# The order in which a weight's norm products take its converted blocks

## The chip, the cores and the metric

The kernel runs on one core of a Trainium2 chip. The metric is the device time of one execution in microseconds, lower is better. Engines are named as in the profile: PE (TensorE, with PEld for its weight loads), DVE (VectorE), ACT (ScalarE), POOL (GpSimd) and SP (SyncE, which issues the DMAs). Each engine works through its own queue of instructions in order.

## The reference

Three stages follow one another. The first is attention that keeps, for each query, the 32 highest scores; the second and the third are two feed-forward layers on its output. The inputs are: q, k, v of 4 batches x 8 heads x 576 tokens x 64; w_gate and w_val 512 x 1536, w_out 1536 x 512, w_in 512 x 2048, w_out2 2048 x 512.

```
scores = q @ k^T / 8;  kept where >= the 32nd largest of the row, else -1e9
attn   = softmax(scores) @ v          -> x, 2304 tokens x 512
x      = (sigmoid(x @ w_gate) * (x @ w_val)) @ w_out
out    = (max(x @ w_in, 0) ** 2) @ w_out2
```

## The kernel before

**Tiling.** The 2304 tokens are 18 tiles of 128 rows, in eleven chunks: four of one tile and seven of two. Attention goes by chunk, by pair of heads, by head and by tile. For each such block PE makes the scores (L281), ACT copies them out of PSUM (L284), DVE finds the 32 largest in four rounds of a maximum and a replacement (L294, L300), POOL and ACT make the masked exponential (L304 to L308), and PE transposes it (L338 or L340) and multiplies it with the values (L373).

**The weights.** They arrive as float64. A weight is cut into blocks of 128 x 512, and two blocks make a pair (6 pairs each for w_gate, w_val and w_out, 8 each for w_in and w_out2; 34 pairs, 68 blocks). `conv` turns a pair into float32: ACT L447 and L466, DVE L461 and L462, POOL L467. When a weight's pairs are there, `scale` looks for a power of two by which the weight can be scaled. It multiplies every 128 columns, cut to bfloat16, with themselves and adds all of that up in one PSUM tile (L484, eight products for each pair, called "the products" below; the trace names the PSUM tile wg_n, wv_n, wo_n, wi_n and, for w_out2, w_n). Then DVE takes the diagonal (L490), PE spreads its sum over the partitions (L492), DVE takes the maximum (L493), and four small DVE steps turn it into the scale. The PSUM tile is one of the two buffers named "wk", which the feed-forward layers' products use too. `split` (L502 to L508) uses the scale to cut the float32 pair into two float16 parts.

**Who needs the result.** Chunk 0 goes through the two layers in plain float32 (`moe32`, L745 to L833) and needs no scale. The other chunks need the split parts (`moe`, L593, L633, L696, L717).

**What sets the order.** The program is written with a priority for each piece of work: attention comes first, then the plain chunk, then the weights' conversions. When the program is built, a planner lays out the instruction order of every engine from these priorities, the dependencies and its own estimated times. On the chip that order is fixed, and each instruction waits on semaphores for what it needs. For w_gate, w_val and w_out `scale` is called right behind the last `conv` of the weight; for w_in and w_out2 it is called between steps of the plain chunk.

Of the kernel before, what the change touches and what calls it, by code (L numbers as in the profile page):

```python
# [19 lines left out]
DRAM = bass.MemoryType.DRAM  # L20

P = 128
# [40 lines left out]
LOA = 0  # L63
# Operands of the split products are scaled by powers of two so that their
# column norms lie below 2**TB; the scales are undone exactly afterwards.
TB = 15
# [3 lines left out]
def tile_topk_attention__then__two_moe_layers(  # L70
# [11 lines left out]
    chunks=None,  # L82
# [7 lines left out]
    KM = DM // P  # L90
# [27 lines left out]

# [1 line left out]
    def pow2_scale(norm, name, pool=mpool, tag=None, bufs=None, squared=True):  # L120
# [13 lines left out]

# [1 line left out]
    kscr = {}  # L136
    kloc = {}

    def prep_keys(b, hp, keep=False):
        """Of two heads: k^T in two parts, each part's rows the heads' one after the other."""  # L140
        src = k[b, 2 * hp : 2 * hp + 2]
        kn = apool.tile([P, S], F32, tag="kn", bufs=1, name=f"kn_{b}_{hp}")
        kv = kn[:, 0 : CB * P].rearrange("p (c h d) -> p c h d", c=CB, h=2)
        for j in range(2):
            nc.sync.dma_start(kv[:, :, j], src[j, 0:SM].rearrange("(p c) d -> p c d", c=CB))
        ke = apool.tile([ST, 2, D], F32, tag="qn", bufs=2, name=f"ke_{b}_{hp}")
        nc.sync.dma_start(ke, src[:, SM:S].rearrange("h p d -> p h d"))
        kh = apool.tile([P, S], F32R, tag="kst", bufs=KST, name=f"kp_{b}_{hp}")
        kl = kn.bitcast(F32R)
        if keep:  # L150
            kl = mpool.tile([P, S], F32R, tag="m4", bufs=M4, name=f"kl_{b}_{hp}")
            kloc[(b, hp)] = (kh, kl)
        for lo, hi in ((0, CB), (CB, NB)):
            pt = ps_t.tile([P, 512], F32, tag="tr", name=f"kpt_{b}_{hp}_{lo}")
            w = 0
            for c in range(lo, hi):
                kp = P if c < CB else ST
                nc.tensor.transpose(
                    pt[:, w : w + kp],
                    (kv[:, c] if c < CB else ke).rearrange("p h d -> p (h d)"),  # L160
                    ident[0:kp, 0:kp],
                )
                w += kp
            c0 = lo * P
            nc.scalar.copy(kh[:, c0 : c0 + w], pt[:, 0:w])
            nc.vector.tensor_tensor(
                kl[:, c0 : c0 + w], pt[:, 0:w], kh[:, c0 : c0 + w], op=ALU.subtract
            )
        d = dpool.tile([2, 2, D, S], F32R, name=f"ks_{b}_{hp}", tag=f"ks_{b}_{hp}")
        for a, t in enumerate((kh.bitcast(F32), kl.bitcast(F32))):  # L170
            for j in range(2):
                nc.sync.dma_start(d.bitcast(F32)[j, a], t[j * D : (j + 1) * D])
        for j in range(2):
            kscr[(b, 2 * hp + j)] = d[j].rearrange("a d s -> (a d) s")

# [1 line left out]
    def pieces(tt):  # L177
# [21 lines left out]
    class Pair:  # L199
        """Two heads of one chunk of tokens."""  # L200

# [37 lines left out]
        def queries(self, tts):  # L239
            for tt in tts:  # L240
# [8 lines left out]
                for b, _, o, n in ps:  # L249
                    # tokens of another batch are zero here  # L250
                    qt = apool.tile([P, 2, 2, P], F32R, tag="qt", bufs=3, name=f"qt_{tt}_{self.hp}_{b}")
                    for p_b, _, o_, n_ in ps:
                        if p_b != b:
                            nc.gpsimd.memset(qt.bitcast(F32)[:, :, :, o_ : o_ + n_], 0.0)
                    sl = slice(o, o + n)
                    nc.scalar.copy(qt[:, 0, :, sl], p3[:, :, sl])
                    nc.vector.tensor_tensor(
                        qt[:, 1, :, sl], p3[:, :, sl], qt[:, 0, :, sl], op=ALU.subtract
                    )
                    self.qt[(tt, b)] = qt  # L260

        def scores(self, j, i):
# [5 lines left out]
            for e in range(2):  # L268
                half = slice(e * HALF, (e + 1) * HALF)
                ops = []  # L270
                for b, _, _, _ in ps:
                    for a in range(2):
                        if self.ci == 0:
                            # both parts still on chip, each head's on its own partitions
                            rows = slice(j * D, (j + 1) * D)
# [11 lines left out]
        def softmax(self, j, i, ss):  # L287
# [26 lines left out]
            if self.ci < DIAG:  # L314
                dg = apool.tile([P, P], F32, tag="we", bufs=3, name=f"dg_{tt}_{h}")
                nc.gpsimd.tensor_scalar(dg, ident, rz, 1.0, op0=ALU.mult, op1=ALU.mult)
                return wk, dg
            # the last keys of both heads lie side by side, to be transposed at once
            if j == 0:
# [5 lines left out]
        def transpose(self, j, i, wk, dg):  # L325
# [8 lines left out]
            for c in range(CB):  # L334
                o, x = tp[:, c * P : (c + 1) * P], wk[:, c * P : (c + 1) * P]
                if self.ci < DIAG:
                    # normalized on the way
                    nc.tensor.matmul(o, x, dg, start=(c == 0), stop=(c == CB - 1), skip_group_check=True)  # L338
                else:
                    nc.tensor.transpose(o, x, ident)  # L340
# [41 lines left out]

# [1 line left out]
    # A float64 weight arrives as its two 32-bit words. The high word, read as a float32,  # L384
    # has the float64's exponent divided by 8 as its own and the rest of it in its mantissa:
    # times 2**-112 it has float32's exponent (what is too small for it becomes zero or next
    # to it), only 3 bits too low. Shifted up, and with its sign and the 3 highest bits of
    # the low word put in, it is the float32.
    REBIAS = float(2.0**-112)
# [10 lines left out]
    nblk = [0]  # L400
    flat = {}  # (name, kt, fb): float32 tile of two blocks, index
    sums = {}
    parts = {}  # (name, kt, fb): tile, index
    scales = {}
# [21 lines left out]
    def conv(name, pi):  # L426
        """Two blocks to float32, and the norms' share of them."""
        pr = pairs_of[name][pi]
# [19 lines left out]
        if wide:  # L448
            for e, r in enumerate(rs):
                hi = r[:, :, 1]  # L450
                if SGN and nblk[0] % SGN == 0:
                    # a zero of the same sign
                    nc.gpsimd.tensor_scalar(
# [20 lines left out]
    def scale(name):  # L474
        """Of a whole weight, from the Gram matrices of its columns, cut to bfloat16, 128 columns
        at a time, all added up: no column's squared norm is above the diagonal's largest entry."""
        gram = ps_w.tile([P, 512], F32, tag="wk", name=f"{name}_n")[:, 0:P]
        n = 0
        for pr in pairs_of[name]:
            c = flat[(name, *pr[0])][0]  # L480
# [56 lines left out]
    def split_act(src, name, xs, N):  # L537
        # src: [P, KM, N]; columns' largest squared norm gives the scale
        sq = xs[:, 1].bitcast(BF16)
# [19 lines left out]

# [1 line left out]
    class Moe:  # L561
# [4 lines left out]
    def start(ci):  # L566
        """The gate and value products of a chunk's first features, ahead of their turn."""
        m = ahead[ci]
# [45 lines left out]
    def moe(ci, nxt=None):  # L614
        """nxt: called before and after the turn from the first layer to the second."""
        m = ahead.pop(ci)
# [3 lines left out]
        def l1_acc(fp, gh):  # L620
            if not accs:
                accs.append(ps_a.tile([P, 2, 512], F32, tag="acc", name=f"acc1_{ci}"))
            acc = accs[0]
            # the last ones bank by bank
            last = fp == NF1 // 2 - 1
# [53 lines left out]
        usc, i2 = layer2_scales()  # L679
        # out = acc2 * (1/(scale of r))**2 / (scale of w_out2)  # L680
        us = mpool.tile([P, 2], F32, tag="us", bufs=2, name=f"us_{ci}")
# [7 lines left out]
        def l2_pair(fp):  # L689
            ph = ps_w.tile([P, 512], F32, tag="wk", name=f"ph_{ci}_{fp}")  # L690
            for e in range(2):
                f0 = (2 * fp + e) * P
                # the low parts of x2 last
                terms = [(c, a, 0) for c in range(KM) for a in range(2)] + [(c, 0, 1) for c in range(KM)]
# [43 lines left out]

# [1 line left out]
    def moe32(ci, xt):  # L740
# [47 lines left out]
        l1_acc(*prev)  # L788
        x2 = xt  # no longer needed
        nc.scalar.copy(x2.rearrange("p d n -> p (d n)"), accs[0][:, 0, 0 : KM * N])  # L790
# [44 lines left out]

# [1 line left out]
    def batches(ci):  # L837
# [9 lines left out]
    up = [0]  # L847

    def attention():
        """Yields once for each block of 128 rows of one head."""  # L850
        units = []
# [44 lines left out]
        def tail(n):  # L896
            pr, pi, j, i = units[n]
            if pr.hp == 0 and pr.ci not in xts:
# [6 lines left out]
                else:  # L905
                    # of a small chunk, its split parts lie in the same tile
                    small = pr.ci in SM2
# [28 lines left out]
    def layer2_scales():  # L936
        if not usc:
            # 1/(scales of w_val, w_out, w_in) and the fixed powers of two between them
            u = const.tile([P, 1], F32, name="usc")
# [25 lines left out]

    # the parts each weight is split into once the plain chunks are done with it
    todo = []  # (least number of steps of the last plain chunk, weight, pair)
    n1 = NF1 // 2
# [109 lines left out]
```

## Time and profile before

| | us |
|---|---|
| median of 3 runs | 1314.05 |
| lowest and highest run | 1313.09, 1314.7 |
| span of the profiled execution, first to last instruction | 1312.3 |
| PE busy in it | 1214.3 (93%) |
| DVE busy | 1018.8 (78%) |
| POOL busy | 838.6 (64%) |
| ACT busy | 758.5 (58%) |
| mean granted TensorE clock | 0.969 of full speed |

The span is that of one profiled execution; the median is 1.75 us above it, and this is taken as what lies around the span. A share of the whole span mixes two stages with different limits, so the stretches are to be read one by one.

### The profile page before, as it was taken

The page shows a single profiled execution, that of the slowest core. Times are in us where ns is not written, and L with a number is a line of the kernel's source. Part 1 is how long each engine was busy: PE and PEld are TensorE (multiplying, and loading weights), DVE is VectorE, ACT ScalarE, POOL GpSimd, SP SyncE. Part 2 cuts the span into 40 slices and gives each one's busy share as a digit, 9 for nine tenths or more (in the row PEclk, how much of TensorE's full clock was granted, in tenths as well). Part 3 has the DMA queues.
Part 4 walks back from the last instruction along what each step waited for, and adds up shares of the span by engine and source line. Part 5 has one row for each costly group of instructions (what it writes and reads, how often), then busy time and mean ns, then how long its engine had stood idle before and what let it go on. Part 6 is the DMA issues. An engine that isn't in the chain of part 4 may idle for free.

```text
span 1312.3 us, 28283 instructions
## 1 busy us (share of the span) xinstructions
PE 1214.3 (93%) x10613; PEld 971.6 (74%) x10613; DVE 1018.8 (78%) x2192; ACT 758.5 (58%) x1500; POOL 838.6 (64%) x1124
## 2 busy tenths in 40 slices
PE   6746798989999899999999999999999999999998
PEld 4535686777978778777888678777876887787775
DVE  6999999999999999989899888985998698210010
ACT  4876767677666665666566655664566566323122
POOL 1988878888676675586567746674576557324223
PEclk9766899999999999999999999999999999999999
DMA  6967861221323221524211233321111110000000
GB/s 187 350 246 252 276 206 56 62 64 54 94 67 103 61 62 28 132 70 137 82 53 36 73 101 96 95 67 53 42 48 42 46 37 10 17 2 1 17 1 16
DMA packets 116328, 113.00 MB, mean 86 GB/s; under 512 B 73440, under 2 KB 87776, under 8 KB 116192
## 3 DMA queue, kind: packets, MB, share of 16 engines
q1 hardware_dynamic: 116192, 111.19, 28.3%
q8 instruction: 84, 1.38, 0.4%
q14 instruction: 52, 0.43, 0.1%
HBM read 96.99 MB, written 14.16 MB: 85 GB/s over the span
## 4 chain that ended last, share of the span: by engine, by line
PE 70%; DVE 14%; POOL 6%; ACT 3%; DMA 3%; issue 3%; SPq 1%; ACTq 0%; POOLq 0%; DVEq 0%
PE acc L717 13%; PE ph L696 12%; PE pg L593 9%; PE pv L593 9%; PE acc L633 9%; PE xp L373 6%; PE sp L281 6%; PE tp L340 4%; DVE mx L294 3%; DVE W L300 3%; POOL W L307 1%; PE qpt L244 1%; DMA wv_r<-in_moe_w_val_dram 1%; DVE wv_c L462 1%; POOL W L322 1%
## 5 line engine op out<-in xcount | busy, mean ns | idle before, releaser
L294 DVE MAX8 mx<-W 128x8 f32<-128x576 f32 x432 | 327.4, 758 | 7.7
L307 POOL TENSOR_TENSOR W<-S,W 128x576 f32<-128x576 f32 x144 | 208.1, 1445 | 32.6 <-ACT W L306 32.1
L696 PE MATMUL ph<-x,wi_w 128*128 128x256 f16 (+1 forms) x1920 | 209.2, 260 | 8.0 <-ACT x L672 7.4
L300 DVE MATCH_REPLACE8 W<-mx,W 128x576 f32<-128x576 f32 x288 | 213.7, 742 | 0.0
L717 PE MATMUL acc<-w_w,rh 128*128 128x512 f16 x816 | 195.8, 379 | 1.5 <-POOL rh L709 1.5
L696 PEld LDWEIGHTS <-wi_w 128*128 128x128 f16 x1920 | 167.2, 99 | 39.7 <-issue 10.4
L306 ACT ACTIVATE W<-S,bs 128x576 f32<-128x576 f32 x144 | 112.0, 778 | 108.2 <-POOL bs L304 107.9
L593 PE MATMUL pg<-xs,wg_w 128*128 128x256 f16 (+1 forms) x1440 | 156.0, 257 | 3.1 <-ACT xs L547 1.6
L308 ACT ACTIVATE W<-W,bs 128x576 f32<-128x576 f32 x144 | 112.0, 778 | 71.8 <-POOL W L307 71.3
L593 PE MATMUL pv<-xs,wv_w 128*128 128x256 f16 (+1 forms) x1440 | 152.7, 257 | 0.2 <-DVE x2cm L668 0.2
L281 PE MATMUL sp<-kst,qt 128*128 128x288 f32 x608 | 130.6, 327 | 9.0 <-ACT S L284 5.0
L593 PEld LDWEIGHTS <-wg_w 128*128 128x128 f16 x1440 | 122.4, 98 | 18.3 <-issue 2.7
L633 PEld LDWEIGHTS <-wo_w 128*128 128x128 f16 x1440 | 123.1, 98 | 16.6 <-issue 3.7
L593 PEld LDWEIGHTS <-wv_w 128*128 128x128 f16 x1440 | 122.7, 98 | 16.4 <-issue 3.3
L717 PEld LDWEIGHTS <-rh 128*128 128x128 f16 x816 | 77.7, 98 | 76.4 <-POOL rh L709 2.0
L605 DVE TENSOR_TENSOR th<-pv,th 128x512 f32<-128x512 f32 (+1 forms) x60 | 36.2, 603 | 119.1 <-PE pv L593 117.9
L633 PE MATMUL acc<-gh,wo_w 128*128 128x256 f16 (+1 forms) x1200 | 124.8, 254 | 2.4 <-POOL gh L609 2.4
L294 DVE MAX8 mx<-S 128x8 f32<-128x576 f32 x144 | 107.4, 746 | 15.7 <-ACT S L284 15.4
L708 POOL TENSOR_TENSOR r<-r 128x512 f32<-128x512 f32 (+1 forms) x80 | 74.7, 936 | 59.8 <-ACT rh L707 58.8
L341 ACT COPY PT<-tp 128x512 f32<-128x512 f32 x144 | 83.7, 581 | 47.6 <-PE tp L340 39.3
L322 POOL TENSOR_SCALAR we<-W,rz 128x64 f32<-128x64 f32 x128 | 41.5, 324 | 108.0 <-DVE rz L313 72.7
L300 DVE MATCH_REPLACE8 W<-mx,S 128x576 f32<-128x576 f32 x144 | 106.8, 742 | 0.3 <-issue 0.3
(297 smaller groups left out, 2224.8 us busy)
## 6 DMA issues: line engine op xcount, KB each, us to landing
kst<-ks SPq DMA_DIRECT2D x104, 288.0 KB, 2.9
v<-in_v_dram SPq DMA_DIRECT2D x112, 128.0 KB, 2.2
qn<-in_q_dram SPq DMA_DIRECT2D x128, 64.0 KB, 2.2
wi_r<-in_moe_w_in_dram SPq DMA_DIRECT2D x16, 512.0 KB, 6.8
w_r<-in_moe_w_out_dram SPq DMA_DIRECT2D x16, 512.0 KB, 4.7
wg_r<-in_moe_w_gate_dram SPq DMA_DIRECT2D x12, 512.0 KB, 8.0
wv_r<-in_moe_w_val_dram SPq DMA_DIRECT2D x12, 512.0 KB, 7.2
wo_r<-in_moe_w_out_dram SPq DMA_DIRECT2D x12, 512.0 KB, 7.0
```

What stands on the lines that cost most here:

```text
L281: nc.tensor.matmul(sp[:, e, 0:HALF], l, r, start=(x == 0), stop=(x == len(ops) - 1))
L294: m8 = nc.vector.max(mx[:, r], cur)
L300: nc.vector.match_replace(wk, mx[:, r], cur, NEG)
L306: nc.scalar.activation(wk, ss, AF.Relu, bias=bs[:, 0:1], scale=-BIG)
L307: nc.gpsimd.tensor_tensor(wk, ss, wk, op=ALU.subtract)
L308: nc.scalar.activation(wk, wk, AF.Exp, bias=bs[:, 1:2], scale=SCALE, accum_out=bs[:, 2:3])
L341: nc.scalar.copy(ptr[:, :, i * P : (i + 1) * P], tp.rearrange("p (c t) -> p c t", c=CB))
L373: nc.tensor.matmul(xp[j * D : (j + 1) * D, o : o + n], vj, pj, start=(si == 0 and c == 0), stop=(c == NB - 1), skip_group_check=True,)
L593: nc.tensor.matmul(pp[:, e * N : (e + 1) * N], wblk(wd, a, c, f0, P), xs[:, b_, c, :], start=(e == 0 and n == 0), stop=(n == 3 * KM - 1), ...
L633: nc.tensor.matmul(acc[:, d // 2, (d % 2) * N : (d % 2 + 1) * N], wblk("wo", a, f, d * P, P), gh[:, b_, e * N : (e + 1) * N], start=(f == ...
L696: nc.tensor.matmul(ph[:, e * N : (e + 1) * N], wblk("wi", a, c, f0, P), x2[:, b_, c, :], start=(e == 0 and n == 0), stop=(n == 3 * KM - 1) ...
L717: nc.tensor.matmul(acc2[:, i, 0:DM], gh[:, b_, e * N + i * P : e * N + (i + 1) * P], wblk("w2", a, f, 0, DM), start=(f == 0 and x == 0), s ...
```

## The change

`scale` walks the pairs of a weight from the last to the first. The products, their number, their operands and their sum's place are the same; the first of a weight's products now reads the pair that is converted last. All other lines of the diff remove comments.

```
     def scale(name):
         gram = ps_w.tile([P, 512], F32, tag="wk", name=f"{name}_n")[:, 0:P]
         n = 0
-        for pr in pairs_of[name]:
+
+        for pr in reversed(pairs_of[name]):
             c = flat[(name, *pr[0])][0]
             m = c.bitcast(BF16).rearrange("p e (f t) -> p (e f) t", t=2)[:, :, 1]
             for f in range(1024 // P):
                 mf = m[:, f * P : (f + 1) * P]
                 nc.tensor.matmul(
                     gram, mf, mf, start=(n == 0), stop=(n == len(pairs_of[name]) * (1024 // P) - 1)
                 )
                 n += 1
```

## Rows read from the trace of the kernel before

**Rows 1.** Stretches: length, busy time (instructions) of each engine, granted clock, DMA.

```profile
core 0: us, PE busy (x) PEld busy (x) DVE busy (x) ACT busy (x) POOL busy (x), PEclk, DMA share, GB/s
27.00:250.00 223.00, 163.55 (x1195) 132.82 (x1195) 216.16 (x375) 158.67 (x300) 188.11 (x159) 0.84 0.64 217
66.00:100.00 34.00, 15.77 (x102) 11.77 (x103) 34.00 (x56) 24.82 (x48) 30.46 (x23) 0.60 0.67 244
...
300.00:1312.00 1012.00, 989.43 (x8765) 786.01 (x8763) 737.52 (x1684) 553.63 (x1114) 606.70 (x902) 1.00 0.20 57
```

**Rows 2.** What PE waited for from 27 to 150 us: total us, times, longest.

```profile
PE wv_n L484 <- POOL wv_c L467: 7.6, 7, 2.3
PE wo_n L484 <- POOL wo_c L467: 6.1, 5, 1.7
PE wg_n L484 <- POOL wg_c L467: 6.0, 5, 2.0
...
PE wv_cb L492 <- DVE wv_d L490: 4.1, 1, 4.1
```

**Rows 3.** What DVE waited for, 27 to 250 us: first and last of six.

```profile
DVE wo_w L505 <- ACT wo_w L502: 2.2, 1, 2.2
...
DVE wg_c L461 <- ACT wg_c L447: 0.4, 1, 0.4
```

**Rows 4.** Timeline of PE: start us, length us, work, idle before, releaser.

```profile
63.91 0.40 PE L484 MATMUL wg_n<-wg_c 128*128 128x128 bf16 x4 [1.09 <-POOL wg_c L467]
...
67.66 2.08 PE L338 MATMUL tp<-dg,W 128*128 128x128 f32 x8 [3.34 <-POOL dg L316]
...
70.93 1.91 PE L484 MATMUL wv_n<-wv_c 128*128 128x128 bf16 x16
...
93.27 0.40 PE L484 MATMUL wv_n<-wv_c 128*128 128x128 bf16 x4 [0.23 <-POOL wv_c L467]
...
99.79 0.26 PE L492 MATMUL wv_cb<-wv_d,ones 128*128 128x128 bf16 x1 [4.13 <-DVE wv_d L490]
...
119.24 0.61 PE L484 MATMUL wo_n<-wo_c 128*128 128x128 bf16 x4 [1.08 <-POOL wo_c L467]
...
143.13 2.00 PE L750 MATMUL pg<-x_plain,wg_c 128*128 128x128 f32 x16
...
180.38 1.76 PE L484 MATMUL wi_n<-wi_c 128*128 128x128 bf16 x28
...
248.11 1.44 PE L593 MATMUL pg<-xs,wg_w 128*128 128x128 f16 x23 [0.65 <-POOL xs L557]
```

**Rows 5.** Timeline of DVE, the diagonal steps L490 of three weights.

```profile
70.55 0.27 DVE L490 TENSOR_TENSOR wg_d<-wg_n,ident 128x128 bf16<-128x128 f32 x1
...
99.47 0.27 DVE L490 TENSOR_TENSOR wv_d<-wv_n,ident 128x128 bf16<-128x128 f32 x1
...
141.00 0.27 DVE L490 TENSOR_TENSOR wo_d<-wo_n,ident 128x128 bf16<-128x128 f32 x1
```

**Rows 6.** By tile: w_in, w_out2; ns min/median/max, first and last start.

```profile
L467 POOL TENSOR_TENSOR wi_c<-wi_c,wi_r x16: 1284/1617/1851, 120.7 to 161.6; 128x512 int32<-128x512 int32 x16
...
L467 POOL TENSOR_TENSOR w_c<-w_c,w_r x16: 1281/1602/2283, 163.3 to 205.1; 128x512 int32<-128x512 int32 x16
...
L484 PE MATMUL w_n<-w_c x64: 217/218/222, 207.0 to 213.3; 128*128 128x128 bf16 x64
```

**Rows 7.** By tile: DVE conversion steps of w_gate, same columns as Rows 6.

```profile
L462 DVE SCALAR_TENSOR_TENSOR wg_c<-wg_r,wg_c x12: 668/678/1899, 33.1 to 58.5; 128x512 uint32<-128x512 uint32 x12
...
L461 DVE TENSOR_SCALAR wg_c<-wg_c x6: 693/886/1668, 31.8 to 55.0; 128x1024 uint32<-128x1024 uint32 x6
```

**Rows 8.** DVE groups from 27 to 250 us: busy us, mean ns, idle before.

```profile
L294 DVE MAX8 mx<-W 128x8 f32<-128x576 f32 x50 | 37.5, 750 | 0.1
...
L462 DVE SCALAR_TENSOR_TENSOR wg_c<-wg_r,wg_c 128x512 uint32<-128x512 uint32 x12 | 11.3, 973 | 0.0
...
L461 DVE TENSOR_SCALAR wg_c<-wg_c 128x1024 uint32<-128x1024 uint32 x6 | 5.9, 990 | 0.4 <-ACT wg_c L447 0.4
```

More of the change, by code (lines that the diff above doesn't have):

```diff
@@ L478, in scale @@
         n = 0
-        for pr in pairs_of[name]:
+        for pr in reversed(pairs_of[name]):
             c = flat[(name, *pr[0])][0]
```

## Prediction

> **What bounds the kernel now.** I read the stretches of the span first, then the waits of PE and of DVE over the stage in which the weights are converted, then the timelines around the products, and at last the durations of DVE's conversion steps.
>
> The stretches [rows 1] show two stages. From 300 us on PE is busy 989.4 of 1012 us at full clock: PE sets the pace there. From 27 to 250 us it is another engine. DVE is busy 216.2 of 223 us, so it is idle for 6.8 us in all; between 66 and 100 us it has no gap at all (34.00 of 34.00). PE in that stretch is busy 15.8 of 34 us, at a granted clock of 0.60. The first stage ends at 248.11, when the first long run of chunk 1's gate products starts, released by POOL's split of chunk 1's input [rows 4]. So the end of the kernel is, roughly, the moment when PE can go on without gaps, plus PE's work left by then. The first of these is set by DVE with POOL close beside it (188.1 of 223 us busy).
>
> The products of w_gate, w_val and w_out lie in the first stage, and PE does wait in them: 6.0 + 7.6 + 6.1 = 19.7 us, each time for POOL's last conversion step L467 [rows 2]. That is the time the edit can hope to give back. DVE's own waits show whether anybody feels it: six entries from 2.2 down to 0.4 us, all behind ACT or POOL, none behind PE [rows 3]. The scores that PE delivers late are still early enough for DVE.
>
> **The change part by part.** *Removed:* products that run while the weight is still being converted. The sum of products is a chain in one PSUM tile, in program order. When the first in the chain reads the last pair, no product can run before that pair is there. Up to now 8 of 48 products of w_gate had to wait for the last pair; now all 48 do, so 40 are moved behind it. The same holds for w_val and w_out; 120 products move in all, each with its weight load. They issue no DMA, so no queue of SP or POOL is passed.
>
> *Price on PE.* A run of 16 products took 1.91 us, one of them at that clock some 0.31: (1.91 - 0.31) / 15 = 0.107 us each at the low clock. A run of 28 took 1.76 us at full clock: (1.76 - 0.22) / 27 = 0.057 us each [rows 4]. So 40 products behind the last pair are 2.3 to 4.3 us, against 19.7 / 3 = 6.6 us of waits for each weight that go. PE's bill is a gain of 2.3 to 4.3 us for each weight, 7 to 13 us over the three, as PE time. As kernel time it is nothing while DVE covers it; without that cover it would be at most DVE's 6.8 us of idle time [rows 1], since DVE can't be fed better than without gaps.
>
> *What stands behind the products on PE.* For w_gate the next work is the transposing of a block, which waited 3.34 us for POOL until 67.66 while the products had ended at 63.91 + 0.40 = 64.31. For w_val the queue ended its products at 93.67, and PE waited 4.13 us for DVE's diagonal step before 99.79 [rows 4]. Both gaps take the 40 products, or nearly. w_out repeats the pattern at 119.24 without such a gap; the work behind it may be 2.3 to 4.3 us later, and DVE has its next scores by then as shown above. I take zero for all three, between a gain of 6.8 us and the loss in the second rival.
>
> *When the norm is needed.* DVE's diagonal step came at 70.55, 99.47 and 141.00 [rows 5], which is 70.55 - 64.31 = 6.24, 99.47 - 93.67 = 5.80 and 141.00 - 119.85 = 21.15 us after the last product. The moved 40 products take 4.3 us of it at most. The splits that read the scales run in the next stage, behind the conversion of the last weight, so the scale being late costs nothing.
>
> *w_in and w_out2.* w_in's last conversion step began at 161.6 and its first product ran at 180.38; the order of pairs can't matter there. For w_out2 the last step began at 205.1 (plus about 1.6 us) and the first product at 207.0 [rows 4, 6]. Nearly no room is left, but the reversed order needs that pair just when the products start, so I take 0, with a bound of 1 us of PE time.
>
> *The sum:* span 1312.3 + 0 = 1312.3, with the 1.75 us around it 1314. That is the median of the runs, and it is my number: 1314.0.
>
> **The rivals.**
>
> *A PSUM buffer that comes free, faster.* The products' sum holds one of the two "wk" buffers. The plain chunk's second group of gate products ran at 143.13, just behind w_out's diagonal step at 141.00 [rows 4, 5], so it may have stood waiting for that buffer, whose sum had been started long before 119.24. With the sum begun late, the plain chunk could go on earlier and clear POOL and DVE around 237 to 248 us. For it: the plain chunk ends only just before chunk 1 starts. Against it: DVE has the same work to do in any case. The gain ends at DVE's idle 6.8 us; half of that gives 1314.05 - 3.4 = 1310.6. Chance 0.10.
>
> *DVE stands at the diagonal step, slower.* DVE works in order. If the planner leaves the diagonal steps where they are and PE takes another block's transposing (2.08 us) and its wait for POOL (3.34 us) ahead of the products [rows 4], then w_gate's sum is ready at 64.31 + 4.3 + 5.4 = 74.0 in place of 64.31, and DVE stands 74.0 - 70.55 = 3.5 us; for w_val, by the same sum, 3.9 us. As DVE is the bound, both are paid: 1314.05 + 7.4 = 1321.5. It decides from the point where products end later than 6.24 (5.80) us after they did. Against it: the planner also sees the later sum and would move the step. Chance 0.11.
>
> *The plan comes out differently, either sign.* The planner orders all engines from its estimates, and the moved products change PE's times from 38 us on. What a step on DVE costs depends on what POOL does beside it. L462 takes 668 ns at its shortest and 1899 at its longest, L461 693 and 1668 [rows 7], with means of 973 and 990, while the maxima of attention average 750 over 50 [rows 8]. Over the shortest, w_gate's 12 and 6 steps cost 12 x 0.305 + 6 x 0.297 = 5.4 us; for all five weights, 68 blocks, that is about 5.4 x 68 / 12 = 31 us of DVE time that hangs on which steps meet. A tenth of it is 3.1 us, a fifth 6.2 us, with no reason for a sign: 1311 or 1317 by a tenth. The Trainium skill, page "SBUF — State Buffer", section "Who interferes with whom", says that a DVE instruction with two SBUF inputs contends with a GpSimd instruction that reads SBUF, by an exclusive lock, so that whoever issues first blocks the other. By that rule a new order alone changes times, and the rows here agree: the two-input L462 spreads from 668 to 1899 ns. Chance 0.23 for faster by more than 0.2%, 0.16 for slower.
>
> *The change does nothing at all.* For w_in and w_out2 it doesn't; for the other three the waits show that it must. This is the forecast's own outcome with another cause, and it shares its time.
>
> **How the numbers follow.** The forecast, waits gone and time unchanged, has a chance of 0.40. Faster by over 0.2% (2.6 us, about what a measurement of this kernel can tell from no change): 0.10 + 0.23 = 0.33. Slower: 0.11 + 0.16 = 0.27. The range goes down to 1314.05 - 6.8 = 1307.2, the bound of DVE's idle time and about a fifth of the meetings, and up to 1314.05 + 6.2 = 1320.3, a fifth of the meetings the other way; what it leaves out is most of the standing DVE and the far ends of the plan, together under 0.2. The likeliest case alone is 1311.4 to 1316.7.
>
> **What would show it.** If I am right, the profile after has the products of w_gate, w_val and w_out each in one or two runs behind the last pair, with no more than one or two waits for POOL in place of 17; PE busy in 27 to 250 us about as before or a little less; DVE still without gaps between 66 and 100 us and with some 7 us of idle time up to 250; chunk 1's gate products starting within 3 us of 248. I am wrong if DVE shows a wait for PE at L490 (slower), if DVE's mean for L461 and L462 moves by a tenth or more (the plan), or if the plain chunk's second group comes well before 143 and chunk 1 starts earlier by as much as the kernel gains (the buffer).

## The result and the profile after

The changed kernel takes 1324.55 us (median of 4 runs, 1324.12 to 1325.32); beside it the kernel before took 1314.38 (4 runs, 1313.09 to 1316.2). The ratio is 1.0078, 95% interval 1.0060 to 1.0095: slower by 10 us, and above the forecast's range (1307.2 to 1320.3). The profiled span grew from 1312.3 to 1323.5 us. After `scale` the line numbers are one higher than before.

The same three stretches as [rows 1], in the same columns:

```profile
27.00:250.00 223.00, 160.47 (x1168) 131.73 (x1167) 213.67 (x373) 159.10 (x299) 186.17 (x157) 0.83 0.65 218
66.00:100.00 34.00, 16.02 (x113) 12.23 (x110) 34.00 (x56) 24.51 (x48) 29.93 (x23) 0.65 0.68 251
300.00:1312.00 1012.00, 989.40 (x8807) 789.43 (x8806) 740.27 (x1693) 554.35 (x1118) 605.04 (x902) 1.00 0.21 56
```

At this grain little moved. DVE has 9.3 us of idle time up to 250 us where it had 6.8, and still no gap from 66 to 100.

What PE waited for from 27 to 150 us, the products' rows of the view of [rows 2]:

```profile
PE wo_n L485 <- POOL wo_c L467: 5.3, 1, 5.3
...
PE wg_n L485 <- POOL wg_c L467: 0.8, 1, 0.8
...
PE wv_n L485 <- POOL wv_c L467: 0.2, 1, 0.2
```

Three waits of 6.3 us in all stand in place of seventeen of 19.7 us. The edit did what it says to the products. PE as a whole did not come free by it: it is busy 160.5 of the 223 us up to 250 us where it was 163.6, so its idle time is 3 us longer.

PE's timeline, as [rows 4]: products of w_gate and w_out, and the start of chunk 1's first long run of gate products:

```profile
64.01 2.70 PE L485 MATMUL wg_n<-wg_c 128*128 128x128 bf16 x44 [0.78 <-POOL wg_c L467]
...
73.13 2.07 PE L338 MATMUL tp<-dg,W 128*128 128x128 f32 x8 [6.42 <-POOL dg L316]
...
120.33 3.06 PE L485 MATMUL wo_n<-wo_c 128*128 128x128 bf16 x30
...
255.50 2.65 PE L594 MATMUL pg<-xs,wg_w 128*128 128x128 f16 x23
```

The products behind the last pair cost 2.70 / 44 = 0.061 and 3.06 / 30 = 0.102 us each, as costed. But chunk 1 starts at 255.50 instead of 248.11: 7.4 of the 11.2 us that the span grew are there before chunk 1's layers have begun. ACT's copy of chunk 1's output comes at 340.34 where it came at 331.45 (+8.9), the last output 11.2 us later than before.

So the trace was followed back from 255.50. The steps that hand chunk 1 over, in order: the last piece of its attention output (ACT L381), the high part of the split on ACT, and the low part in two steps on POOL. Timelines of ACT and of POOL before:

```profile
235.53 0.26 ACT L381 COPY x_plain<-xp 128x128 f32<-128x128 f32 x1
...
244.33 0.70 ACT L547 ACTIVATE xs<-x_plain,x_1s 128x512 f16<-128x512 f32 x1
...
253.86 0.58 ACT L832 COPY ob<-acc 128x512 f32<-128x512 f32 x1
```

```profile
245.15 1.67 POOL L556 TENSOR_SCALAR x_plain<-x_plain,x_1s 128x512 f32<-128x512 f32 x1
246.90 1.16 POOL L557 TENSOR_TENSOR xs<-x_plain,xs 128x512 f16<-128x512 f32 x1
```

and after:

```profile
240.63 0.27 ACT L381 COPY x_plain<-xp 128x128 f32<-128x128 f32 x1 [0.89 <-PE xp L373]
...
247.40 0.56 ACT L833 COPY ob<-acc 128x512 f32<-128x512 f32 x1
...
250.09 0.72 ACT L548 ACTIVATE xs<-x_plain,x_1s 128x512 f16<-128x512 f32 x1
```

```profile
250.29 1.42 POOL L307 TENSOR_TENSOR W<-S,W 128x576 f32<-128x576 f32 x1 [0.52 <-ACT W L306]
251.69 0.33 POOL L322 TENSOR_SCALAR we<-W,rz 128x64 f32<-128x64 f32 x1
251.98 0.70 POOL L557 TENSOR_SCALAR x_plain<-x_plain,x_1s 128x512 f32<-128x512 f32 x1
252.65 1.67 POOL L322 TENSOR_SCALAR W<-W,rz 128x512 f32<-128x512 f32 x1
254.28 1.16 POOL L558 TENSOR_TENSOR xs<-x_plain,xs 128x512 f16<-128x512 f32 x1
```

The attention output is 5.1 us later, ACT's part 5.8 and POOL's last step 7.4, since in POOL's queue steps of the next chunk's attention now stand ahead of the two steps of the split (until 252.0, where ACT's part was done at 250.8) and between them. The plain chunk, on the other hand, comes earlier: ACT copies out its output (`ob`) at 247.40 where it did at 253.86. The new plan brings chunk 0 forward by 6.5 us and puts chunk 1's start back by 7.4.

The 5.1 us arise between 126 and 152 us. PE's timeline before and after, around the transposes (`kpt`) of keys of the second batch, which only later chunks use (the kernel makes them ahead, during chunk 1's attention), the plain chunk's products (`pg`, `acc`) and the scores (`sp`) of attention block 11 (blocks counted from 0; 8 to 15 are chunk 1's):

```profile
126.26 1.11 PE L158 MATMUL kpt<-ident,kn 128*128 128x128 f32 x4
127.31 0.35 PE L158 MATMUL kpt<-ident,ke 64*128 64x64 f32 x1
127.58 1.38 PE L750 MATMUL pg<-x_plain,wg_c 128*128 128x128 f32 x10
...
132.91 1.16 PE L338 MATMUL tp<-dg,W 128*128 128x128 f32 x8 [2.16 <-POOL dg L316]
...
137.64 3.72 PE L772 MATMUL acc<-g,wo_c 128*128 128x128 f32 x16 [1.17 <-DVE g L762]
141.07 0.81 PE L281 MATMUL sp<-kst,qt 128*128 128x288 f32 x4
141.72 1.05 PE L338 MATMUL tp<-dg,W 128*128 128x128 f32 x8
```

```profile
127.40 1.38 PE L751 MATMUL pg<-x_plain,wg_c 128*128 128x128 f32 x10 [1.71 <-ACT x_plain L381]
...
130.18 0.60 PE L158 MATMUL kpt<-ident,kn 128*128 128x128 f32 x4
...
135.52 2.05 PE L338 MATMUL tp<-dg,W 128*128 128x128 f32 x8 [4.12 <-DVE kn L166]
...
142.09 3.79 PE L773 MATMUL acc<-g,wo_c 128*128 128x128 f32 x16 [1.74 <-DVE g L763]
145.67 1.60 PE L338 MATMUL tp<-dg,W 128*128 128x128 f32 x8
...
148.71 0.77 PE L281 MATMUL sp<-kst,qt 128*128 128x288 f32 x4
```

The key transposes went behind the plain chunk's products, the next transposing waited 4.1 us for DVE's step on them, and the scores of block 11 came 7.6 us later: 4.5 us are there at the plain chunk's products `acc`, and the rest comes behind them, where another block's transposing (145.67) now stands ahead of the scores. DVE meanwhile wasn't idle, it did something else. Its timeline after:

```profile
145.14 2.55 DVE L461 TENSOR_SCALAR wi_c<-wi_c 128x1024 uint32<-128x1024 uint32 x2
147.61 4.81 DVE L462 SCALAR_TENSOR_TENSOR wi_c<-wi_r,wi_c 128x512 uint32<-128x512 uint32 x4
152.34 0.28 DVE L494 TENSOR_REDUCE wocx<-wo_cb 128x1 f32<-128x128 f32 x1
152.54 0.74 DVE L294 MAX8 mx<-S 128x8 f32<-128x576 f32 x1
```

Seven microseconds of w_in's conversion, which the plain chunk needs and chunk 1's start doesn't, then block 11, at 152.54 where it began at 144.77. DVE began it 3.1 us after its scores left PE, and 2.9 us before, so the conversion filled the time of the late scores and added little of its own. A full DVE hid the loss from every view of busy time.

### The profile page after: what moved, and what is told of

Its sections match the earlier page's. It is cut to its first block, busy times and chain, and to the rows that moved or that the text cites. A ratio compares the mean times of both kernels' runs of the same rounds, so it can differ in the third digit from the quotient of the medians.

```text
span 1323.5 us, 28308 instructions
## 1 busy us (share of the span) xinstructions
PE 1216.4 (92%) x10613; PEld 975.7 (74%) x10613; DVE 1017.1 (77%) x2192; ACT 760.8 (57%) x1500; POOL 837.3 (63%) x1124
## 4 chain that ended last, share of the span: by engine, by line
PE 68%; DVE 13%; POOL 7%; ACT 5%; issue 3%; DMA 2%; SPq 1%; ACTq 0%; POOLq 0%; DVEq 0%
PE acc L718 13%; PE ph L697 13%; PE pg L594 8%; PE pv L594 8%; PE acc L634 8%; PE xp L373 6%; PE sp L281 5%; DVE mx L294 4%; PE tp L340 4%; DVE W L300 3%; POOL W L307 2%; PE qpt L244 1%; ACT W L306 1%; ACT W L308 1%; DVE wv_c L462 1%
## 5 line engine op out<-in xcount | busy, mean ns | idle before, releaser
L697 PEld LDWEIGHTS <-wi_w 128*128 128x128 f16 x1920 | 164.5, 98 | 41.1 <-issue 11.4
L281 PEld LDWEIGHTS sp<-kst,qt 128*128 128x128 f32 x608 | 91.8, 194 | 27.7 <-ACT S L284 10.4
```

The costliest lines, as they stand in the source:

```text
L281: nc.tensor.matmul(sp[:, e, 0:HALF], l, r, start=(x == 0), stop=(x == len(ops) - 1))
L697: nc.tensor.matmul(ph[:, e * N : (e + 1) * N], wblk("wi", a, c, f0, P), x2[:, b_, c, :], start=(e == 0 and n == 0), stop=(n == 3 * KM - 1) ...
```

## The experiments

Two theories were on trial first. **A, the place of the products:** 120 products behind the last pairs delay PE's other work, each weight by its share. **B, the plan:** the products cost nothing, but the planner, seeing other times for PE, orders all engines anew, and the new order is worse. The medians of before beside these runs were 1312.6 to 1313.6 us. "Start" below is that of chunk 1's first long gate run (248.11 before, 255.50 after).

**One weight at a time.** In `scale`, the pairs reversed for one name alone (w_val and w_out likewise; `last_first`: the last pair first and the others forward, which leaves the same products behind the last pair):

```
-        for pr in pairs_of[name]:
+        for pr in pairs_of[name][::-1] if name in ('wg',) else pairs_of[name]:
# last_first:
+        for pr in pairs_of[name][-1:] + pairs_of[name][:-1]:
```

> Only w_gate's pairs are taken in reverse. In the instruction order that the planner makes of it, DVE differs from the kernel before in a few swaps between about 40 and 80 us and is the same from there on; ACT, POOL and SP likewise. Theory A (the place of the products: 40 of them stand behind the last pair, PE gets to attention later, each weight pays its share of the loss): about a third of the 10 us, 1317 to 1318.5. Theory B (the plan: the loss is made by another order of all engines far behind the products): within 2.6 us of before, 1312 to 1317, and the blocks of attention from the tenth on at the times of before.

> Only w_val's pairs are taken in reverse. The planner's order differs from before on every engine from there to the end. Theory A: again about a third of the loss, 1317 to 1318.5. Theory B: any time within some 12 us of before on either side, with no tie to the share of 3 us; chunk 1's first long run of gate products moves from 248 by about what the kernel gains or loses.

> Only w_out's pairs are taken in reverse. The planner's order differs from before on every engine from there to the end. Theory A: a third or more of the loss, 1317 to 1319, and the three single weights add up to about 10 us. Theory B: any time within some 12 us of before, and the three don't add up to the loss of the whole change.

> The last pair first, then the others from the first on, for all weights: the same wait as in the change with another order behind it. The planner's order on DVE, ACT, POOL and SP is the same as that of the change, and PE's differs only in which pair a product reads. Both theories: the time of the change, 1322 to 1327. A time near that of before would mean that the order of the pairs themselves matters, which neither theory has.

| kernel | us | ratio [95%] | start |
|---|---|---|---|
| rev_wg | 1313.77 | 1.0002 [0.9993, 1.0011] | 247.9 |
| rev_wv | 1328.8 | 1.0113 [1.0099, 1.0127] | 259.1 |
| rev_wo | 1320.01 | 1.0044 [1.0031, 1.0058] | 256.3 |
| last_first | 1324.49 | 1.0078 [1.0065, 1.0091] | 256.0 |

Forty products of w_gate behind its last pair cost nothing, and its plan is that of before from some 80 us on. w_val alone costs more than the whole change. No sum of shares gives that (0.0 + 1.1 + 0.4 against 0.78), so A is in trouble. `last_first`, whose orders on DVE, ACT, POOL and SP are those of the change, has its time to 0.1 us.

**Other nudges of the plan.** `cols_rev` keeps the pairs forward and turns only the eight column groups of a pair, so nothing moves behind the last pair; `delay_x1` leaves the products alone and gives POOL four multiplications by 1 on chunk 1's input, 2.8 to 6.7 us of work; `dve_x1_fwd` and `dve_x1_rev` make chunk 1's low part by one step of DVE in place of two of POOL, in the kernel before and in the changed one.

```
# cols_rev
-            for f in range(1024 // P):
+            for f in reversed(range(1024 // P)):
# delay_x1
+        for _ in range(4 if ci == 1 else 0):
+            nc.gpsimd.tensor_scalar(xt, xt, 1.0, 1.0, op0=ALU.mult, op1=ALU.mult)
# dve_x1_fwd, dve_x1_rev
+        if ci == 1:
+            nc.vector.scalar_tensor_tensor(xs[:, 1], xt, sx, xs[:, 0], op0=ALU.mult, op1=ALU.subtract)
+            return xs, ix
```

> Pairs from the first to the last as before, but the eight column groups inside a pair from the last to the first. Only 4 of a pair's 8 products move, behind 4 others of the same pair; none goes behind the last pair. The planner's order on DVE parts from that of before at its 57th row, and on every engine after it. Theory A (the place of the products makes the loss): within 2.6 us of before. Theory B (any change of the planner's order can cost or give several us through the start of chunk 1): off by up to 12 us either way, and the first long run of chunk 1's gate products off 248 us by about the same.

> The kernel before with four more POOL steps on chunk 1's input (a multiplication by 1, 0.7 to 1.7 us each by the same step in before, 2.8 to 6.7 us in all) between the two steps that split it. DVE's planned order is the one of before up to its 359th row, so the early stage is untouched and chunk 1 starts later. Theory B: the kernel gets longer by about what chunk 1's start moves, 1316 to 1321. A rival, that a later start of chunk 1 is made good behind it because attention runs ahead meanwhile: within 2.6 us of before.

> The kernel before with chunk 1's low parts made by one DVE step in place of two POOL steps (1.67 and 1.16 us, and a step of the plain chunk of 0.6 ahead of them); the early stage is untouched. Theory B: chunk 1 starts some 2 us earlier and the kernel ends 1.5 to 3 us earlier, 1310.5 to 1312. The rival: no change.

> The changed kernel with the same DVE step in place of the two POOL steps for chunk 1. There the POOL steps ran at 252.0 and 254.3 behind other work, 255.4 at the end, while ACT's high part was ready at 250.8. Theory B: chunk 1 starts 3 to 4 us earlier than in the changed kernel and the kernel gains as much, 1320 to 1322; the later attention of chunk 1 remains. If the loss lay somewhere behind chunk 1: 1324.5.

| kernel | us | ratio [95%] | start |
|---|---|---|---|
| cols_rev | 1327.3 | 1.0100 [1.0082, 1.0118] | 255.0 |
| delay_x1 | 1324.75 | 1.0081 [1.0065, 1.0097] | 256.6 |
| dve_x1_fwd | 1324.62 | 1.0077 [1.0057, 1.0097] | - |
| dve_x1_rev | 1320.67 | 1.0051 [1.0032, 1.0069] | 253.2 |

`cols_rev` moves no product behind the last pair and loses 1%. `delay_x1` loses more than the work it adds, and `dve_x1_fwd`, meant to be faster, loses 0.8%; the same edit on the changed kernel gains 3 to 4 us. (No start is given for `dve_x1_fwd`: its one profiled execution took 4199 us.) The forecasts for `delay_x1` and `dve_x1_fwd` missed: both went by the start of chunk 1 alone. Every kernel so far whose order differs from before's past the first 80 us ends 7 to 15 us later than before.

**The one swap on PE.** With the local cause in view, the planner was told of it: the plain chunk's gate products go on, from their fourth on, only behind the key transposes (an order, not a wait), in the changed kernel, in `rev_wv` and in `cols_rev`. `rev_wi_w2` went with them as a control. (The lines that note the two products' instructions are left out.)

```
+                    if pr.hp == 1:
...
+                        tc.add_manual_dep(pg0[3].ins, kpt_last[0].ins.name, NOSYNC, reason="keys first")
```

> The changed kernel with one ordering condition for the planner and no other edit: the plain chunk's gate products may go on, from the fourth on, only after the transposes of chunk 1's last pair of keys, as they stood in the kernel before (transposes at 126.3, gate products at 127.6 us; changed: 127.4 and 130.2). Theory B1 (this swap on PE makes attention block 11 of chunk 1 about 8 us late, and that lateness is the loss): block 11 starts by 146, chunk 1's long run of gate products by 251, time 1313 to 1318. Rival B2 (the swap is one of many; the plan comes out late in another place): block 11 or a later block still late, the long run at 253 or later, time 1320 to 1328.

> The kernel with only w_val's pairs reversed (1328.8, ratio 1.0113; long run of chunk 1's gate products at 259.1, block 11 at 154.6) with the same ordering condition. B1: block 11 by 147, long run by 252, time 1314 to 1319. B2: long run after 255, time 1322 or more.

> Pairs forward, the eight column groups within a pair reversed (1327.3, ratio 1.0100; long run at 255.0, block 11 at 153.8), with the same ordering condition. B1: block 11 by 147, long run by 251, time 1314 to 1319. B2: long run after 253, time 1321 or more.

> The kernel before with the pairs of w_in and w_out2 alone reversed: the planned orders of DVE, ACT, POOL and SP are those of the kernel before, only PE's products stand elsewhere. Theory B (the order of the other engines is what costs): 1312 to 1315, ratio within 0.2% of 1, long run of chunk 1's gate products at 247 to 249. Rival (the place of products on PE costs by itself): 1316 or more.

The keys are called chunk 1's in the first of these; they are those of the second batch, as said above. Of its two times for the changed kernel the first is that of the gate products, the second that of the transposes.

| kernel | us | ratio [95%] | start | block 11 |
|---|---|---|---|---|
| kpt_first_rev | 1322.19 | 1.0072 [1.0058, 1.0086] | 254.5 | 144.5 |
| kpt_first_wv | 1328.85 | 1.0124 [1.0106, 1.0141] | 260.3, in two parts | 155.3 |
| kpt_first_cols | 1320.34 | 1.0061 [1.0048, 1.0073] | 248.6 | 147.3 |
| rev_wi_w2 | 1312.67 | 0.9998 [0.9989, 1.0007] | 248.0 | 144.6 |

B1, the swap as the one cause, falls. In `kpt_first_rev` block 11 is back on time, and only 1 to 2 of 10 us return. The last attention output of chunk 1 comes at 239.05, still 3.5 us late, and then POOL's timeline has this:

```profile
249.44 1.12 POOL L508 TENSOR_SCALAR wi_c<-wi_c,wis 128x1024 f32<-128x1024 f32 x1
250.54 0.69 POOL L557 TENSOR_SCALAR x_plain<-x_plain,x_1s 128x512 f32<-128x512 f32 x1
251.20 2.12 POOL L509 TENSOR_TENSOR wi_w<-wi_c,wi_w 128x1024 f16<-128x1024 f32 x1
253.29 1.15 POOL L558 TENSOR_TENSOR xs<-x_plain,xs 128x512 f16<-128x512 f32 x1
```

A split of w_in stands ahead of and between the two steps that PE waits for. In `kpt_first_cols` even the start is back (248.6), and 7 us are still lost, by the end of chunk 2 (ACT's copy of its output at 411.6; before 404.0). Take one late event away and another stands in its place. `rev_wi_w2`, in which only PE's products of two weights stand elsewhere, costs nothing.

**Orders pinned.** Now the two suspects were separated outright. A list (`ORDER`, left out here) holds the order in which a planned kernel has each engine's instructions; each is tied to the one before it, with no wait:

```
+    for seq in ORDER:
+        for a, b in zip(seq, seq[1:]):
+            tc.add_manual_dep(by[f"I-{b}"], f"I-{a}", NOSYNC, reason="order of before")
```

> The changed kernel, with ordering conditions for the planner (no waits) that keep every instruction of DVE, ACT, POOL and SP, and PE's except the norm products themselves, in the order of the kernel before; the planner places only the reversed products among them. Theory B (the planned order of all engines is what costs, the products' own order nothing): 1312 to 1316, ratio within 0.2% of 1, chunk 1's long run of gate products at 247 to 249. Rival A (the reversed products cost by themselves): 1320 or more.

> The mirror: the kernel before, with its products' pairs forward, but every other instruction kept in the order of the changed kernel. Theory B: 1321 to 1328, the long run at 254 to 257. Rival A: 1316 or less, since the products stand as before.

> The changed kernel with DVE's order alone kept as before; PE, ACT, POOL and SP are planned freely round it. If it is DVE's choice between conversions and attention that makes chunk 1 late: 1312 to 1317, block 11 by 147, long run by 250. If other engines' orders cost as much: 1319 or more.

> The changed kernel with PE's order alone kept as before (but for the products); DVE, ACT, POOL and SP are planned freely round it. If PE's swap of the key transposes and the plain chunk's gate products is the root, and the rest follows from it: 1312 to 1318, block 11 by 147. If DVE's own order costs: 1320 or more.

In the traces DVE's, ACT's and POOL's instructions, and PE's other than the products, stand in `pin_rev` in exactly the order of before, and in `pin_fwd` in exactly that of the change.

| | orders of before | orders of the change |
|---|---|---|
| products forward | before: 1 | pin_fwd: 1.0079 [1.0065, 1.0092], 1324.03 us |
| products reversed | pin_rev: 0.9997 [0.9989, 1.0006], 1312.77 us | the change: 1.0078 [1.0060, 1.0095] |

The start of chunk 1 on PE's timeline, in `pin_rev` and then in `pin_fwd`:

```profile
247.91 1.45 PE L593 MATMUL pg<-xs,wg_w 128*128 128x128 f16 x23 [0.66 <-POOL xs L557]
```

```profile
255.76 1.77 PE L593 MATMUL pg<-xs,wg_w 128*128 128x128 f16 x23
```

That settles A against B. The products' order costs 0.0%, in either plan; the order of everything else costs all 0.8%. One engine's order alone does not carry it: DVE's kept as before gives 1322.39 (1.0063 [1.0047, 1.0078]), PE's 1324.32 (1.0079 [1.0065, 1.0093]). In the latter the start is only 3.7 us late (251.85) and the rest is lost behind it. In the former (`pin_rev_dve`) chunk 1 starts at 257.24, later than in the change itself, and DVE is idle for 16.5 us up to 250 us, though it has its instructions in exactly the order of before. This is its row and that of `pin_rev`, in the columns of [rows 1]:

```profile
27.00:250.00 223.00, 158.08 (x1144) 131.40 (x1144) 206.54 (x355) 152.15 (x287) 176.59 (x150) 0.82 0.66 216
```

```profile
27.00:250.00 223.00, 163.07 (x1196) 133.95 (x1197) 216.42 (x376) 159.05 (x300) 187.84 (x160) 0.86 0.65 217
```

So DVE's choice of what comes first is not the cause by itself; it is the orders of the engines together.

**Which half of the plan.** Two hybrids switch from one plan's orders to the other's at chunk 1's first gate product.

> The changed kernel, each engine's order kept as in the change up to chunk 1's first gate product, and from there on as in the kernel before. If the loss is laid down in the first stage: the long run at 254 to 257, time 1320 to 1326. If what follows the first stage in the change's plan costs as much: 1314 to 1318.

> The mirror, also on the changed kernel: orders as before up to chunk 1's first gate product, from there on as in the change. If the loss is laid down in the first stage: the long run at 247 to 249, time 1312 to 1317. If the later order costs: 1319 or more.

`hyb_change_then_before` takes 1318.95 us (1.0053 [1.0039, 1.0067]), starting at 254.1, a time between the two readings of its expectation; `hyb_before_then_change` 1323.98 (1.0086 [1.0072, 1.0100]), starting at 257.7, which neither reading of its expectation had. Its attention output is only 1.6 us late, but then POOL:

```profile
246.72 1.66 POOL L556 TENSOR_SCALAR x_plain<-x_plain,x_1s 128x512 f32<-128x512 f32 x1
...
251.27 0.21 POOL L305 TENSOR_SCALAR bs<-mx 128x1 f32<-128x1 f32 x1 [2.01 <-DVE rz L312]
252.65 1.42 POOL L307 TENSOR_TENSOR W<-S,W 128x576 f32<-128x576 f32 x1 [1.18 <-ACT W L306]
...
256.04 1.17 POOL L557 TENSOR_TENSOR xs<-x_plain,xs 128x512 f16<-128x512 f32 x1
```

Between the split's two steps the later order of the change puts attention work of the next chunk, waits for DVE and ACT included; the second step begins 9.3 us after the first, where in the kernel before it was 1.8 us. The halves' losses, 6.3 and 11.4 us, don't add up to the change's 10.2. It may be that an order fits the other half of its own plan; no run shows that by itself. Ahead of before's later order the first stage's order costs 6 us; what makes up the rest lies at the handover or behind it, and how it divides there stays open. No plan that the runs tried beats the kernel before, so there is no better version to show.

## Why the prediction was wrong

**What it had right, and one reading that it had not.** The products' waits for POOL go (19.7 to 6.3 us, three in place of seventeen). They did not become PE time, though, as the "gain of 2.3 to 4.3 us for each weight" has it. In `pin_rev`, where all else keeps its order, the products wait for 2.6 us, and PE is busy 163.1 us up to 250 us, as before (163.6): it waits as long as before, behind other steps. Two entries that were 5.5 and 3.1 us before, from 27 to 150 us, are in `pin_rev`:

```profile
PE tp L338 <- POOL dg L316: 10.7, 3, 7.4
PE sp L281 <- ACT S L284: 10.0, 3, 6.7
```

The price on PE, forecast as 0.057 to 0.107 us for a product, was 0.061 and 0.102. The norm is needed late enough: w_gate's sum ends at 64.01 + 2.70 = 66.71 and DVE's diagonal step runs at 73.0. No wait of DVE for PE appears there, so the standing DVE (rival two) did not occur. Nor did the first rival's sign, the plain chunk's second group of gate products well before 143 us: it ran at 147.62. w_in and w_out2 cost nothing (0.9998). `pin_rev` measures the sum itself: with the other orders held, the edit is worth 0.0%, as the 1314.0 said.

**The step that failed** is in the first part, "What bounds the kernel now", and in the sum that rests on it: the first stage's end was taken as "set by DVE", as if DVE's total work fixed it, and the sum, "span 1312.3 + 0", had no term for the order that the planner would draw anew. That a gain or loss on PE is "nothing while DVE covers it" held where the other orders were kept: `pin_rev` costs 0.0%. The term left at nothing is the new order, and `pin_fwd`, with the old products, measures it as 0.79%, 10.4 us. DVE's total work does not say when chunk 1 is handed over; that depends on the order of the work on all engines. From 27 to 250 us DVE's busy time fell by 2.5 us and its idle time rose by as much, while the handover went from 248.11 to 255.50. In the change's trace the scores of attention block 11 came 7.6 us later, with w_in's conversion in their place on DVE, and POOL's split then stood behind the next chunk's attention. Neither event carries the loss alone: with block 11 back in time (`kpt_first_rev`) most of it stays, and with DVE's own order kept (`pin_rev_dve`) chunk 1 starts at 257.24. Which differences between the two orders make the loss stays open. The sign "chunk 1's gate products starting within 3 us of 248" is the one that failed.

**The rival that happened** is the third, the plan that comes out differently, with 0.16 on the slow side. That the planner draws another order was right; its price was made of the wrong thing. It was priced by how often DVE's conversion steps meet POOL's; all 102 steps L461 and L462 together took 98.0 us before and 98.6 after (single weights moved more: w_in's L462 from 12.6 to 15.1 us, w_out's L461 from 8.4 to 6.1). That is 0.6 us in all, not the 3 to 6 us that were allowed, and the sign given for this rival, a mean moved by a tenth, did not come, so on this case's rows the rule cited there from the Trainium skill, page "SBUF — State Buffer", section "Who interferes with whom", gives no account of the loss. Nor was it "no reason for a sign": eleven of the kernels above, the change among them, were planned freely, or with the one condition on the keys, into an order that differs past the first 80 us, and all eleven lost 7 to 15 us (three of them also change a little work of chunk 1's split, and `last_first` has the orders of the change). The plan of before is a good one among these neighbours, and a range with 6 us upwards for a new plan was too short.

## What to carry to other kernels

Where a planner orders all engines from its estimates, an edit's own price and the price of the order that it draws are two numbers; tie all other instructions to the old order to read the first, and the old code to the new order to read the second. A view of busy time hides a change in what comes first, so ask of each stage what its successor waits for and follow that chain, here attention output, ACT's part, POOL's two steps, rather than totals of busy time. When one late event is mended and the time stays, look at the whole order before looking for the next event.

## What was not expected of the hardware

Around the handover TensorE's granted clock differs between the profiled executions, even of two kernels whose instructions, but for the products, have one order (the change and `pin_fwd`). These are the stretches from 250 to 260 us before, after and in `pin_fwd` (columns as in [rows 1]):

```profile
250.00:260.00 10.00, 10.00 (x131) 8.41 (x130) 9.83 (x19) 6.85 (x14) 8.13 (x11) 1.00 0.32 102
```

```profile
250.00:260.00 10.00, 8.33 (x59) 7.08 (x58) 9.73 (x20) 6.18 (x11) 9.55 (x11) 0.53 0.22 61
```

```profile
250.00:260.00 10.00, 8.33 (x74) 6.88 (x75) 9.73 (x20) 6.61 (x12) 9.32 (x11) 0.68 0.22 61
```

After, PE had waited 2.73, 0.60 and 1.08 us ahead of its scores between 246 and 254 us; the clock granted is 0.53 of full speed, mostly the 1.2 GHz level, and the run of 23 products takes 2.65 us, where it took 1.44 before at 1.00 and 1.77 in `pin_fwd` at 0.68. In `pin_fwd` PE had waited nearly the same (2.74, 0.60 and 1.07 us), and yet the clock came back earlier. The medians of the change and of `pin_fwd` agree to 0.5 us, but one profiled execution of each does not say what the longer dip costs, and what a dip costs against none at all was not measured apart.
